# Two attention blocks on one core: another opening, zero matmuls, and the output projection from unit 40 at 2.5 matmuls a unit

## The chip, the cores and the metric

The kernel runs on one core of a Trainium2 chip. The time is that of one execution on the device, in microseconds; a kernel's time is the median of its runs. The profile is one further execution, taken by the hardware profiler. Its engines are TensorE (PE, with its weight loads PEld), VectorE (DVE), ScalarE (ACT), GpSimd (POOL) and SyncE (SP); SPq and POOLq are the queues in which SyncE and GpSimd issue DMAs.

## The reference

Two independent problems A and B of the same shape, with their own inputs, all bf16. For each, 16 batches of 144 query rows of width 448, 16 heads of width 256, and a cache of 512 keys and values per batch and head:

```python
q = (x @ wq).reshape(B, Sq, H, Dh).transpose(0, 2, 1, 3)      # x 16x144x448, wq 448x4096
scores = jnp.einsum("bhqd,bhkd->bhqk", q, k_cache) * (Dh ** -0.5)
p = softmax(scores, axis=-1)
o = jnp.einsum("bhqk,bhkd->bhqd", p, v_cache)
y = o.transpose(0, 2, 1, 3).reshape(B, Sq, H * Dh) @ wo       # wo 4096x448
out = concatenate([y_A, y_B], axis=-1)
```

## The kernel before

**Units.** A unit is one batch and one head of one problem; there are 2 x 16 x 16 = 512, in order of problem, batch and head. A unit goes through these steps, each named in the code by a letter pair and the unit's number:

- Q: eight matmuls of 128x144 make the unit's queries, transposed, in one PSUM bank (`t_q`); ScalarE or VectorE scales them into `qt_sb` (`t_evac_q`). Q of unit u stands `LQ` = 15 slots ahead of the unit.
- SA: two matmuls of 112x512 make the scores of the first 112 query rows, in one of two banks `sa_ps` (`t_sa`). VectorE takes the negated maximum (L436), ScalarE the exponential with its sum (L447), VectorE the reciprocal (L457), GpSimd multiplies (L465). Then TA: four transposes through TensorE into the same bank (`t_ta`), which VectorE copies to `pt_sb` (L488). SA stands `LS` = 5 slots ahead of its unit, TA 2.
- SB: the remaining 32 query rows of eight units are done together, in 16 small matmuls into the two banks `sb_ps` (`t_sb`), once in eight slots, 7 slots ahead. Their softmax runs for four units at a time; TB are their transposes.
- PV: eight matmuls of 128x144 of values and probabilities into one of two banks `ot_ps` (`t_pv`); ScalarE copies the result into a ring of four chunks of 128 output rows (`t_evac_ot`).
- OP: the output projection of a chunk of 128 rows is 32 matmuls of 128x448 into `op_ps` (`t_op_piece`). A chunk is complete when all 16 heads of its batches are; there are 18 chunks for each problem. ScalarE copies a finished chunk to `ost_sb` and GpSimd issues its store (`t_store`). The two last chunks run in `op_ps` and `qp_ps` together, and VectorE copies the second.

**Order.** A loop over slots i writes every engine's instructions in one fixed order; slot i holds PV of unit i and the earlier steps of later units. `_Sched.add` records each instruction with what it reads and writes, and puts in the semaphore waits. Within a slot TensorE has Q, SB (once in eight), SA, TA, TB (twice in eight), PV, OP.

**How OP is dealt out.** A finished chunk's 32 matmuls go into a queue with the slot from which they may run (two slots after the unit that completes it). Each slot adds `OP_RATE` to a credit (18 x 32 / 256 = 2.25), and matmuls are taken in pairs while a credit of one is left. While both queues are empty the credit is capped at four. After a chunk's last matmul no further one of that queue is taken until two slots later (`op_hold`).

**Loads.** All loads are issued by SyncE, in the order of a list sorted by due slot (`dma_plan`): x (transposed, for four batches), Wq in four groups of four heads, K for eight units (2 MB, transposed by the DMA, three buffers), V for four units (1 MB, three buffers), Wo in eight groups of four row blocks. A load that would overwrite a buffer waits on SyncE for the last reader, and everything behind it in the list waits too. Before, the list begins: x0, three groups of Wq, K0, the fourth Wq, V0, K1, V1, V2, K2, a Wo group, V3, two Wo groups, V4, K3, and Wo goes on until K5. V9, V10, K6, V11 follow. Wo of problem B is loaded as the last chunk of A releases each group.

The lines that deal out OP and cap the credit:

```python
            if i >= 0:
                credit += OP_RATE
            ...
            for bank in ("op", "qp"):
                while fifo[bank] and fifo[bank][0][2] <= i and credit >= 1 and (bank == "qp" or i >= op_hold):
                    r, cs = pop_items(bank, i, OPP)
                    credit -= len(cs)
            ...
            if not fifo["op"] and not fifo["qp"]:
                credit = min(credit, 2.0 * OPP)
```

Of the kernel before, what the change touches and what calls it, by code (L numbers as in the profile page):

```python
# [122 lines left out]
def bass_concat_heads__mha_block_cached__gqa_block_cached__near_ridge_kernel(  # L123
# [38 lines left out]
    LSB = 7  # L162
    NK, NV, NXG = 3, 3, 3
# [3 lines left out]
    KR = 4  # L167
# [8 lines left out]
    with contextlib.ExitStack() as es:  # L176
# [29 lines left out]
        sem_names = list(COMPUTE)  # L206
# [23 lines left out]
        def t_ident():  # L230
# [7 lines left out]
            S.add(POOL, e2, reads=[("ones", 0)], writes=[("ident", 0)], name="ident")  # L238

# [63 lines left out]

        def t_q(U):
# [4 lines left out]
            hg = h // 4  # L309

            def e(t):
                ins = None
                for kc in range(4):
                    for dc in range(2):
                        c0 = h * DH + dc * 128
                        ins = t.matmul(qp_ps[:, dc * SQ:(dc + 1) * SQ], lhsT=wq_sb[:, kc, c0:c0 + 128],  # L316
                                       rhs=xt_sb[:, xsl, kc, xo:xo + SQ], start=(kc == 0 and dc == 0),
                                       stop=(kc == 3), skip_group_check=True)
                return ins
            S.add(PE, e, reads=[(("wq", hg), pr), ("wqz", 0), (("xt", xsl), XG)], writes=[("qp", ("q", U))],  # L320
                  banks=["qp"], name="Q%d" % U)

        def t_evac_q(U):
            sl = U % NQT
            src = qp_ps[:, 0:2 * SQ].rearrange("p (c q) -> p c q", c=2)
            if (U - LQ) % 8 in (2, 4, 6, 7):
                def e(v):
                    return v.tensor_scalar(qt_sb[:, sl, :, :], src, 1.0 / 16.0, None, op0=ALU.mult)  # L328
                S.add(DVE, e, reads=[("qp", ("q", U))], writes=[(("qt", sl), U)], banks=["qp"], name="eq%d" % U)
            else:  # L330
                def e(a):
                    return a.activation(qt_sb[:, sl, :, :], src, AF.Copy, scale=1.0 / 16.0)  # L332
                S.add(ACT, e, reads=[("qp", ("q", U))], writes=[(("qt", sl), U)], banks=["qp"], name="eq%d" % U)
# [5 lines left out]
        def t_sb(SG):  # L339
            ksl = SG % NK  # L340

            def e(t):
                ins = None
                for dc in range(2):
                    for jj in range(8):
                        U = 8 * SG + jj
                        j = jj % 4
                        ins = t.matmul(sb_ps[jj // 4][32 * j:32 * j + 32, :].rearrange("q (k r) -> q k r", k=KR),  # L348
                                       lhsT=qt_sb[:, U % NQT, dc, QA:SQ],
                                       rhs=kt_of(U, dc), start=(dc == 0), stop=(dc == 1),  # L350
                                       tile_position=(0, 32 * j))
                return ins
            S.add(PE, e, reads=[(("qt", (8 * SG + jj) % NQT), 8 * SG + jj) for jj in range(8)] + [(("kt", ksl), SG)],
                  writes=[(("sbb", 0), ("s", 2 * SG)), (("sbb", 1), ("s", 2 * SG + 1))], banks=["sb0", "sb1"],
# [115 lines left out]
        def t_ta(U):  # L470
            psl = U % NPA
            bank = U % 2
# [10 lines left out]
        def t_evac_pta(U):  # L483
            sl = U % NPT
            bank = U % 2
# [87 lines left out]
        def t_store(r):  # L573
            pr, row0, m = chunk_rows(r)
            sl = r % NOST

            def e(q):
                return q.dma_start(of[row0:row0 + m, pr * D:(pr + 1) * D], ost_sb[0:m, sl, :]).then_inc(
                    sems["ost%d" % sl], 16)
            S.add(POOL, e, reads=[(("ost", sl), r)], dma_sem="ost%d" % sl, name="st%d" % r)  # L580
# [4 lines left out]
        t_ident()  # L585
        dma_plan = []
# [4 lines left out]
        s_min = -LQ - 24  # L591
        for XG in range(NXGT):
            pr, j = divmod(XG, Bn // XB)
            u_first = pr * NU + j * XB * H
            dl = u_first - LQ
# [6 lines left out]
        for pr in range(NP):  # L602
            for hg in range(HG):
                dl = pr * NU + 4 * hg - LQ
                lo = pr * NU - H + 4 * hg + 3 - LQ + 1 if pr > 0 else s_min
                plan(lo, dl, 10 ** 6, t_load_wq, pr, hg)
        for wg in range(NWG):
            plan(s_min, H - 4 + 2 * wg, 10 ** 6, t_load_wo, 0, wg)
        for SG in range(NSG):
            dl = 8 * SG - LSB  # L610
            lo = 8 * (SG - NK) + 7 - LS + 1 if SG >= NK else s_min
            plan(lo, dl, 12, t_load_k, SG)
        for G in range(NG):
            dl = 4 * G
# [5 lines left out]
        for dl, sq, lo, lead, fn, args in dma_plan:  # L620
            _prev = max(_prev, lo, dl - lead)
# [20 lines left out]
        OP_RATE = float(NCH * NWO) / NU  # L642
# [16 lines left out]
        while True:  # L659
# [3 lines left out]
            sgi, ph = divmod(i + LSB, 8)  # L663
            do_sb = ph == 0 and 0 <= sgi < NSG
            ga, gb = 2 * sgi, 2 * sgi + 1
            ok = 0 <= sgi < NSG
            if ok and ph == 1:
                t_exp_b(ga)
            if ok and ph == 3:
                t_exp_b(gb)  # L670
            if ok and ph == 2:
                t_recip_b(ga)
                t_norm_b(ga)
            if ok and ph == 4:
                t_recip_b(gb)
                t_norm_b(gb)
# [131 lines left out]
```

## Time and profile before

| | |
|---|---|
| median of 3 runs | 1211.84 us (1211.61 to 1212.8) |
| the profiled execution | 1210.82 us |
| its span, first to last instruction | 1209.1 us |
| TensorE busy | 1174.4 us, 97% |
| VectorE, ScalarE, GpSimd busy | 770.1, 753.7, 678.5 us |
| moved by DMA | 294.15 MB, mean 243 GB/s |
| first Q, first SB, first PV start | 10.33, 23.69, 37.88 us |
| SB of units 8, 16, 24, 32, 40, 48, 56 start | 39.11, 56.49, 73.76, 94.47, 112.87, 132.48, 148.94 us |
| last matmuls, last stores issued | 1201.99, 1203.09 us |

SB(n) is the one for units 8n to 8n+7; it stands in slot 8n - 7. How to read it: the page has busy times of engines and the costliest groups; a list of waits says who waited for whom and how long in total and at most; the timeline gives the start and duration of an instruction or of several alike. A matmul's duration holds its passage through the array, so consecutive groups overlap, and their spacing by start times is what they take. A DMA view gives the time from issue to landing; start of the issue plus that time is the landing.

### The profile page before, as it was taken

The page shows a single profiled execution, that of the slowest core. Times are in us where ns is not written, and L with a number is a line of the kernel's source. Part 1 is how long each engine was busy: PE and PEld are TensorE (multiplying, and loading weights), DVE is VectorE, ACT ScalarE, POOL GpSimd, SP SyncE. Part 2 cuts the span into 40 slices and gives each one's busy share as a digit, 9 for nine tenths or more (in the row PEclk, how much of TensorE's full clock was granted, in tenths as well). Part 3 has the DMA queues.
Part 4 walks back from the last instruction along what each step waited for, and adds up shares of the span by engine and source line. Part 5 has one row for each costly group of instructions (what it writes and reads, how often), then busy time and mean ns, then how long its engine had stood idle before and what let it go on. Part 6 is the DMA issues. An engine that isn't in the chain of part 4 may idle for free.

```text
span 1209.1 us, 33868 instructions
## 1 busy us (share of the span) xinstructions
PE 1174.4 (97%) x13952; PEld 894.2 (74%) x13952; DVE 770.1 (64%) x2179; ACT 753.7 (62%) x2213; POOL 678.5 (56%) x682
## 2 busy tenths in 40 slices
PE   4898999999999999999999999999999999999997
PEld 3676777777777777777777777777777777777765
DVE  1765666666666666666666666666666666666563
ACT  1665666666666666666666666666666666666553
POOL 0555565565555565565555655655655655665553
PEclk9999999999999999999999999999999999999999
DMA  9999999999999999999999999998999999999971
GB/s 249 281 285 289 245 252 225 245 251 247 246 235 237 231 259 226 246 246 232 290 283 282 284 272 265 228 258 225 245 244 236 224 249 244 242 240 234 232 178 47
DMA packets 627033, 294.15 MB, mean 243 GB/s; under 512 B 548416, under 2 KB 556608, under 8 KB 626880
## 3 DMA queue, kind: packets, MB, share of 16 engines
q1 hardware_dynamic: 625152, 287.85, 101.8%
q0 software_dynamic: 1728, 4.13, 1.1%
q8 instruction: 111, 1.82, 0.6%
q14 instruction: 42, 0.34, 0.1%
HBM read 148.90 MB, written 4.13 MB: 127 GB/s over the span
## 4 chain that ended last, share of the span: by engine, by line
PE 90%; DMA 5%; DVE 3%; SPq 1%; ACT 0%; issue 0%; POOL 0%; ACTq 0%
PE qp_ps L316 20%; PE ot_ps L511 19%; PE sa_ps L424 19%; PE op_ps L549 17%; PE sa_ps L478 8%; PE sb_ps L348 5%; DMA kt_sb<-in_A_k_cache_dram 3%; PE sb_ps L401 2%; DMA kt_sb<-in_B_k_cache_dram 2%; DVE stat L436 1%; DMA wq_sb<-in_A_wq_dram 0%; DVE pt_sb L488 0%; PE qp_ps L549 0%; DVE pt_sb L410 0%; DVE qt_sb L328 0%
## 5 line engine op out<-in xcount | busy, mean ns | idle before, releaser
L465 POOL TENSOR_TENSOR pa_sb<-pa_sb,stat 112x512 bf16<-112x512 bf16 x512 | 531.8, 1039 | 490.8 <-DVE stat L457 490.7
L447 ACT ACTIVATE pa_sb<-sa_ps,stat 112x512 bf16<-112x512 f32 x512 | 352.1, 688 | 408.0 <-DVE stat L436 407.0
L436 DVE TENSOR_REDUCE stat<-sa_ps 112x1 f32<-112x512 f32 x512 | 353.9, 691 | 324.6 <-PE sa_ps L424 321.1
L316 PE MATMUL qp_ps<-xt_sb,wq_sb 128*128 128x144 bf16 x4096 | 344.1, 228 | 16.1 <-DMA wq_sb<-in_A_wq_dram 10.3
L316 PEld LDWEIGHTS qp_ps<-xt_sb,wq_sb 128*128 128x128 bf16 x4096 | 290.5, 99 | 93.1 <-issue 11.1
L511 PE MATMUL ot_ps<-pt_sb,v_sb 128*128 128x144 bf16 x4096 | 340.4, 226 | 0.0
L424 PE MATMUL sa_ps<-kt_sb,qt_sb 128*112 128x512 bf16 x1024 | 310.9, 385 | 1.0 <-DVE pt_sb L488 0.8
L549 PE MATMUL op_ps<-wo_sb,ring 128*128 128x448 bf16 x1120 | 278.8, 352 | 0.0
L511 PEld LDWEIGHTS ot_ps<-pt_sb,v_sb 128*128 128x128 bf16 x4096 | 268.5, 97 | 0.4
L478 PEld LDWEIGHTS sa_ps<-ident,pa_sb 112*128 112x128 bf16 x2048 | 145.0, 97 | 111.3 <-ACT pa_sb L447 24.9
L526 ACT ACTIVATE ring<-ot_ps 128x288 bf16<-128x288 f32 (+8 forms) x512 | 190.3, 372 | 4.4 <-PE ot_ps L511 4.4
L488 DVE COPY pt_sb<-sa_ps 128x448 bf16<-128x448 bf16 x512 | 190.7, 372 | 2.4 <-PE sa_ps L478 2.4
L478 PE MATMUL sa_ps<-ident,pa_sb 112*128 112x112 bf16 x2048 | 185.4, 212 | 0.1
L328 DVE TENSOR_SCALAR qt_sb<-qp_ps 128x288 bf16<-128x288 f32 x256 | 117.0, 457 | 96.5 <-PE qp_ps L316 93.9
L389 POOL TENSOR_TENSOR pb_sb<-pb_sb,stat 128x512 bf16<-128x512 bf16 x128 | 132.8, 1037 | 27.1 <-DVE stat L381 27.1
L332 ACT ACTIVATE qt_sb<-qp_ps 128x288 bf16<-128x288 f32 x256 | 106.0, 414 | 35.0 <-PE qp_ps L316 32.5
L424 PEld LDWEIGHTS sa_ps<-kt_sb,qt_sb 128*112 128x112 bf16 x1024 | 97.0, 129 | 38.8 <-issue 26.7
L549 PEld LDWEIGHTS op_ps<-wo_sb,ring 128*128 128x128 bf16 x1120 | 95.1, 98 | 27.6 <-ACT ring L526 0.2
L447 ACT ACTIVATION_READ_ACCUMULATOR pa_sb<-sa_ps,stat 112x1 f32 x512 | 98.9, 193 | 0.0
L361 DVE TENSOR_REDUCE stat<-sb_ps 128x1 f32<-128x512 f32 x128 | 87.2, 681 | 3.7 <-PE sb_ps L348 3.7
L371 ACT ACTIVATE pb_sb<-sb_ps,stat 128x512 bf16<-128x512 f32 x128 | 88.5, 691 | 0.0
L457 DVE RECIPROCAL stat<-stat 112x1 f32<-112x1 f32 x512 | 78.4, 153 | 0.5 <-ACT pa_sb L447 0.5
(23 smaller groups left out, 366.1 us busy)
## 6 DMA issues: line engine op xcount, KB each, us to landing
v_sb<-in_A_v_cache_dram SPq DMA_DIRECT2D x64, 1024.0 KB, 6.1
v_sb<-in_B_v_cache_dram SPq DMA_DIRECT2D x64, 1024.0 KB, 6.0
out_dram<-ost_sb POOLq DMA_DIRECT2D x36, 112.0 KB, 5.1
wo_sb<-in_A_wo_dram SPq DMA_DIRECT2D x8, 448.0 KB, 6.3
wo_sb<-in_B_wo_dram SPq DMA_DIRECT2D x8, 448.0 KB, 6.2
wq_sb<-in_A_wq_dram SPq DMA_DIRECT2D x4, 768.0 KB, 6.7
wq_sb<-in_B_wq_dram SPq DMA_DIRECT2D x4, 768.0 KB, 7.6
wq_sb<-in_A_wq_dram SPq DMA_DIRECT2D x4, 128.0 KB, 6.9
```

What stands on the lines that cost most here:

```text
L316: ins = t.matmul(qp_ps[:, dc * SQ:(dc + 1) * SQ], lhsT=wq_sb[:, kc, c0:c0 + 128], rhs=xt_sb[:, xsl, kc, xo:xo + SQ], start=(kc == 0 and dc ...
L328: return v.tensor_scalar(qt_sb[:, sl, :, :], src, 1.0 / 16.0, None, op0=ALU.mult)
L389: return g.tensor_tensor(pb_sb[:, psl, :], pb_sb[:, psl, :], stat[:, RINVB + sl:RINVB + sl + 1].to_broadcast([128, SK]), op=ALU.mult)
L424: ins = t.matmul(sa_ps[bank][0:QA, :].rearrange("q (k r) -> q k r", k=KR), lhsT=qt_sb[:, U % NQT, dc, 0:QA], rhs=kt_of(U, dc), start=(dc = ...
L436: return v.tensor_reduce(stat[0:QA, NEG + sl:NEG + sl + 1], sa_ps[bank][0:QA, :], axis=AX.X, op=ALU.max, negate=True)
L447: return a.activation(pa_sb[0:QA, psl, :], sa_ps[bank][0:QA, :], AF.Exp, bias=stat[0:QA, NEG + sl:NEG + sl + 1], scale=1.0, accum_out=stat ...
L465: return g.tensor_tensor(pa_sb[0:QA, psl, :], pa_sb[0:QA, psl, :], stat[0:QA, RINV + sl:RINV + sl + 1].to_broadcast([QA, SK]), op=ALU.mult)
L478: ins = t.transpose(pta_ps[bank][:, c * 128:c * 128 + QA], src[:, c, :], ident[0:QA, 0:QA])
L488: return v.tensor_copy(pt_sb[:, sl, :, 0:QA], pta_ps[bank][:, 0:512].rearrange("p (c q) -> p c q", c=4)[:, :, 0:QA])
L511: ins = t.matmul(ot_ps[ob][:, dc * SQ:(dc + 1) * SQ], lhsT=v_sb[:, vsl, j, c * DH + dc * 128:c * DH + (dc + 1) * 128], rhs=pt_sb[:, sl, c, ...
L526: ins = a.activation(ring[:, 2 * h:2 * h + 2, c0:c0 + n1], src[:, :, 0:n1], AF.Copy)
L549: ins = t.matmul(acc[0:m, 0:D], lhsT=ring[:, c, col0:col0 + m], rhs=wo_sb[:, c, :], start=(c == first), stop=(c == last))
```

## The change

- The loads begin with x0, two groups of Wq, K0, the two other groups of Wq, V0, V1, V2, K1, K2. The first slot is now -9 instead of -39, and these loads carry due slots below -50, which puts them first.
- Q of the first 32 units no longer stands 15 slots ahead of its unit, but in slots of a table (`q_slot`): eight in slot -6, four in -3, four in -1, the others in 4 to 16. The first eight use four PSUM banks in turn (`qp_ps`, `op_ps` and the two `ot_ps`), the next 24 use `qp_ps` and `op_ps`. SB0, SB1 and SB2 move to slots -5, 4 and 10, SA of unit 8 to slot 4.
- Twelve zero matmuls of 128x512 stand before the first Q (W0) and 28 between the eighth Q and SB0 (W1). They read the identity and a part of `pt_sb` that VectorE clears, and write a bank that SB0 overwrites.
- Loads of problem A's Wo are due from slot 36 on, 1.7 slots apart, instead of from slot 12 on, 2 apart. In the list three groups stand between K5 and K6 (with V9 and V10), two more before V11, and three after V11.
- Chunks of problem A may run from unit 40 on; those of B as before. `OP_RATE` is 10/9 of what it was, 2.5.
- The two last stores are issued by SyncE, behind its last load, instead of GpSimd, with semaphores of their own, and SyncE waits for them at its end.

```diff
+    OP_FROM = (40, 0)
+    N_WARM = (12, 28)
...
+        def t_warm_zero():
+            def e(v):
+                return v.memset(pt_sb[:, 0, :, :], 0.0)
+            S.add(DVE, e, writes=[("warm", 0)], name="warmz")
...
+        def q_bank(U):
+            four = ((qp_ps, "qp", "qp"), (op_ps, "opp", "op"), (ot_ps[0], ("otp", 0), "ot0"),
+                    (ot_ps[1], ("otp", 1), "ot1"))
+            if U < 8:
+                return four[U % 4]
+            return four[U % 2] if U < 32 else four[0]
...
+        def t_warm(k):
+            def e(t):
+                ins = None
+                for _ in range(N_WARM[k]):
+                    ins = t.matmul(sb_ps[1][:, :], lhsT=ident[:, :], rhs=pt_sb[:, 0, :, 0:128], start=True, stop=True)
+                return ins
...
-            S.add(POOL, e, reads=[(("ost", sl), r)], dma_sem="ost%d" % sl, name="st%d" % r)
+            S.add(SP if r in tail_chunks else POOL, e, reads=[(("ost", sl), r)], dma_sem=sem, name="st%d" % r)
...
+        sb_slot = [8 * n - LSB for n in range(NSG)]
+        sb_slot[0:3] = [-LS, 4, 10]
+        sa_slot = [u - LS for u in range(NT)]
+        sa_slot[8] = 4
+        q_slot = [u - LQ for u in range(NT)]
+        q_slot[0:32] = [-6] * 8 + [-3] * 4 + [-1] * 4 + [4, 5, 5, 6, 7, 8, 9, 9] + \
+            [10, 11, 11, 12, 13, 14, 15, 16]
...
-        s_min = -LQ - 24
+        s_min = -LS - 4
...
-                dl = pr * NU + 4 * hg - LQ
+                dl = pr * NU + 4 * hg - LQ if pr > 0 else (-59, -58, -56, -55)[hg]
...
-            plan(s_min, H - 4 + 2 * wg, 10 ** 6, t_load_wo, 0, wg)
+            plan(s_min, OP_FROM[0] - 4 + 1.7 * wg, 10 ** 6, t_load_wo, 0, wg)
...
-            dl = 8 * SG - LSB
+            dl = 8 * SG - LSB if SG > 2 else (-57, -51, -50)[SG]
...
-            dl = 4 * G
+            dl = 4 * G if G > 2 else -54 + G
...
-        OP_RATE = float(NCH * NWO) / NU
+        OP_RATE = 10.0 / 9 * NCH * NWO / NU
...
+            if i == q_slot[0]:
+                t_warm(0)
+            for u in q_at.get(i, ()):
                 t_q(u)
                 t_evac_q(u)
+            if i == q_slot[0]:
+                t_warm(1)
...
-                            queue_chunk(r, i + OP_DELAY)
+                            queue_chunk(r, max(i + OP_DELAY, pr * NU + OP_FROM[pr]))
...
+                if eng_name == SP:
+                    for k in range(len(tail_chunks)):
+                        eng.wait_ge(sems["ostt%d" % k], 16)
```

## The prediction

> **What bounds the kernel now.** I read the page's shares first, then TensorE's waits and the DMA queue's own, then the timeline where TensorE is full and where it is not.
>
> ```profile
> PE 1174.4 (97%) x13952; PEld 894.2 (74%) x13952; DVE 770.1 (64%) x2179; ACT 753.7 (62%) x2213; POOL 678.5 (56%) x682
> DMA  9999999999999999999999999998999999999971
> ```
>
> TensorE and DMA both look full, so the waits must say which one ends last. TensorE's waits (total, times, longest):
>
> ```profile
> PE qp_ps L316 <- DMA wq_sb<-in_A_wq_dram: 10.3, 1, 10.3
> PE sb_ps L348 <- DMA kt_sb<-in_A_k_cache_dram: 6.1, 4, 1.9
> PE sb_ps L348 <- DMA kt_sb<-in_B_k_cache_dram: 2.9, 2, 2.2
> ```
>
> SyncE's queue, which issues every load:
>
> ```profile
> SPq L301 <- PE op_ps L549: 239.3, 58, 12.8
> ```
>
> After the start TensorE waits 9.0 us in all for K, in the opening (56 to 113 us) and at the change of problem, while the loads wait 239 us for TensorE to free V buffers. So the opening is bound by loads, the rest by TensorE's order. Three consecutive units there, by the start of PV:
>
> ```profile
> 158.74 0.66 PE L511 MATMUL ot_ps<-pt_sb,v_sb 128*128 128x144 bf16 x8
> 160.75 0.67 PE L511 MATMUL ot_ps<-pt_sb,v_sb 128*128 128x144 bf16 x8
> 162.76 0.67 PE L511 MATMUL ot_ps<-pt_sb,v_sb 128*128 128x144 bf16 x8
> ```
>
> 2.01 us a unit, with two out-projection matmuls. The chain of waits gives these a price, 4.16/22 = 0.189 us each:
>
> ```profile
> 1170.32 4.16 PE op_ps L549 x22
> ```
>
> So a unit without out-projection has 2.01 - 0.378 = 1.632 us of TensorE work. A stretch without any (1150 to 1168 us) shows what such a unit takes:
>
> ```profile
> 1160.50 0.64 PE L424 MATMUL sa_ps<-kt_sb,qt_sb 128*112 128x512 bf16 x2
> ...
> 1162.28 0.64 PE L424 MATMUL sa_ps<-kt_sb,qt_sb 128*112 128x512 bf16 x2
> ```
>
> ```profile
> 1161.18 0.69 DVE L436 TENSOR_REDUCE stat<-sa_ps 112x1 f32<-112x512 f32 x1 [0.33 <-PE sa_ps L424]
> 1161.85 0.38 DVE L488 COPY pt_sb<-sa_ps 128x448 bf16<-128x448 bf16 x1
> ```
>
> 1.78 us. SA feeds VectorE's maximum, the copy that frees the other score bank stands behind that maximum on VectorE, and the next SA waits for the copy: 0.64 + 0.61 + 0.07 + 0.38 and the hand-overs. This loop is a floor: an empty unit costs TensorE 1.78 - 1.632 = 0.148 us of idling, while a unit with out-projection covers it. The first empty unit after a full one takes 1.69, 0.055 over. Check: the sixteen units whose SB stand at 148.94 and 185.00 took 36.06 us with 32 out-projection matmuls and one run of six empty units; the same work at the dense rate (18.02 us per eight units with 18) is 35.28, and 0.055 + 5 x 0.148 = 0.80 makes up the rest.
>
> The end, by the lines of the epilogue:
>
> ```profile
> L176 SPq DRAIN  x1: 128/128/128, 1178.7 to 1178.7; - x1
> L176 POOLq DRAIN  x1: 3006/3006/3006, 1205.9 to 1205.9; - x1
> ```
>
> The last stores, issued by GpSimd at 1203.09, land at 1205.6; only then does GpSimd drain, and the drain ends the span.
>
> **The change, part by part.**
>
> *Opening: order of loads, banks, zero matmuls.* K0 stands ahead of the third Wq group instead of behind it: it landed at 7.34 + 16.2 = 23.6 and moves up by that group's 2.9 (landings 13.5 and 16.4), to 20.7. SB0 starts then, 3 us earlier. The third and fourth Wq then land at about 25 and 28 (the fourth came 4.4 behind K0, a group takes 2.9). Three V at 2.7 to 3.7 now stand before K1, which landed at 39.0 and moves to 43 to 46; K2 has the same loads ahead of it as before and stays near 56. Four banks remove the waits of Q for one bank (3.1 + 2.6 us). The zero matmuls (12 and 28, of 512 columns; SA's pair holds the array 0.43 us, so 0.215 each) take 2.6 and 6.0 us, twice that at the slow rate seen in the opening, where eight Q matmuls show 1.14 us and later 0.67. The first batch lies in the 10.3 us before Wq, the second before K0; slow, it holds SB0 to 31.5. The memset that they read is 288 words wide, an eighth of 2048 in the 1.76 us row: 0.25 us on an idle VectorE. I cost all this at nothing. What hides it is first the wait for K1, then a longer one at unit 40; without that cover it would be worth -3 to +8 us, as SB0 moves.
>
> *Wo from unit 36.* Eight Wo loads (1.15 us each between landings) leave the stretch before K5. K5 landed at 94.03 + 18.7 = 112.7 and moves to about 103.5.
>
> *Out-projection from unit 40.* Between SB1 and unit 40 every unit is now empty: 15.8 us per eight with SB (1.11) and two TB (0.45). From K1 at 44.5, six units and eight Q make 13.5 (SB2 58), seven units and eight Q 14.5 (72.5), then 88.3 and 104.1 (SB5), so TensorE comes to unit 40 at about 118. Chunk 0 sits in the queue from unit 15, so the cap on the credit no longer applies and the credit grows by 2.5 a unit to over 60: all 32 matmuls of chunk 0 stand at unit 40, and all 32 of chunk 1 at unit 42. Chunk 0 needs all eight Wo groups. SyncE issues three before K6, two after it, three after V11. Up to the last of them the set of loads is exactly the one that the kernel before had issued up to V11, which landed at 125.31 + 6.0 = 131.3, with the DMA engines never idle until then. The last Wo group therefore lands at 131.3 as well, and TensorE stands 6 to 7 us in the middle of chunk 0, with SB6 and all later units queued behind.
>
> Chunk 0 then ends near 132, and SB6 starts at 132.5, where it starts now (132.48). But by then the kernel before has done 58 out-projection matmuls, the changed one 32: 26 x 0.189 = 4.9 us of work is moved out of a stretch where TensorE had waited for loads anyway. By SB7 both have done 64: 8 x 1.632 + 1.11 + 0.45 + 32 x 0.189 + 0.85 for seven empty units = 21.5, so SB7 at 154.0 against 148.94. **+5.0 us.** Ends: -3.3 if loads run at the best rates of the rows (first rival); +9.1 if SyncE is held once on the way by a V buffer that isn't free (239.3 us in 58 waits, 4.1 each). I take the equal set of loads, since no such wait stands before 125 us now.
>
> *Rate 2.5 instead of 2.25.* A chunk is ready every sixteen units. Before: 10, 4, 2, 2, 2, 2, 2, 2, 2, 4 matmuls and six empty units; after: 12, 2, 2, 4, 2, 2, 2, 4, 2 and seven. Every eighth batch adds a ninth chunk, whose backlog fills some hundred units at 2.25 and about fifty at 2.5; then the empty runs return. Counted in the recorded orders, units 50 to 497 hold 31 first empty units in either kernel, and 42 later ones before, 110 after. 68 x 0.148 = **+10.1 us**. Ends: 68 x 0.055 = +3.7 by the first-unit row; 10.1 itself, which I take, because these stand second to seventh in their runs, as the units of the row do. Nothing offsets it: total out-projection work is equal.
>
> *Stores of the two tail chunks from SyncE.* GpSimd ends with its last multiplication near 1197 and drains before the stores land; SyncE waits for both, and its drain is 0.13 us. 3.0 - 0.13 = **-2.9 us**, if a store from SyncE lands 2.0 us after issue as GpSimd's does. Ends: 0, if SyncE's drain with stores behind it is as long as GpSimd's, and -3.4. The Trainium skill, "DMA: Bandwidth & Descriptors", section Specifications, gives a first byte after about 1 us for DMAs of GpSimd and 0.6 for SyncE's; by that the term would be -3.3 and the sum 11.8. No row here has a store from SyncE.
>
> **Sum.** 5.0 + 10.1 - 2.9 = +12.2 us. The profiled execution took 1210.82 (span 1209.1 and 1.7 around it), so 1223.0; the median of the runs is 1.0 above it, so **1224.0**.
>
> **The rivals.**
> - A: the opening isn't held by Wo. Rows for it: K took 7.2 us between landings at best, V 2.7; seven K, twelve V, eight Wo and Wq would be in by 111. Then K1 43.3, SB5 102.2, SB6 124.1, SB7 145.6: -3.3 in place of +5.0, total +3.9, 1215.7. Against it: in the same queue K took 8.5 to 9.9 whenever V and K alternated.
> - B, on the other side: loads, not TensorE's order, set the pace everywhere. DMA's row of nines speaks for it, SyncE's 239 us of waits against. Then where out-projection stands costs nothing, both positive terms go, and K2, with fewer changes between kinds of load, may come 1.4 early: -1.4 - 2.9 = -4.3, 1207.5. It decides once loads need more than 18.0 us per eight units; K to K with two V was 15.1 (landings 112.7 and 127.9).
> - C: the stall at unit 40 makes TensorE slow again. In the opening eight Q and SB0 (1.90 against 1.05) and one more Q lost 9 x 0.47 + 0.85 = 5.1 us so. Once more after the stall: 1229.1. Against it: SBs after waits of 1.5 to 1.9 us took 1.05. The Trainium skill, "TensorE: Matmul & The Clock Gate", section "HAM oscillation", says that idle gaps over about 3.4 us bring the slow clock back; by that, an estimate, 3.4 us at half rate, +1.7. The trace agrees that the opening is slow and later short waits are not.
>
> **How the numbers follow.** My forecast 0.79, A 0.08, B 0.06, C 0.07. A measurement of this kernel tells 0.2% (2.4 us) from no change. B is faster (0.05, and 0.01 so weak that it is same); 0.03 of A and of my forecast with the steady term at its low end fall within: faster 0.05, same 0.04, slower 0.91. Range 1215 to 1230: from A to C with the late Wo.
>
> **What would show it.** A wait of OP in unit 40 for Wo, ending near 131; SB6 near 132.5 and SB7 near 154; runs of seven empty units at 1.78; no POOL drain behind the stores. The forecast is wrong if Wo is in before unit 40, if empty units take 1.63, or if SB comes to wait for K throughout.

## The result, and the profile after

The changed kernel took 1233.87 us (median of six runs, 1229.02 to 1235.92), the kernel before, run beside it, 1212.43 (1211.61 to 1215.53): 1.017 times as long, 95% interval 1.0149 to 1.019. The profiled execution of the changed kernel took 1233.81 us, its span is 1232.1. Forecast were 1224.0 and a range up to 1230: the sign was right, the size was not.

The page of the changed kernel shows hardly more than before: TensorE full, DMA full. New is what the second line below shows, the granted TensorE clock in tenths: it falls below nine in the slice from 123 to 154 us, where the kernel before had nine throughout.

```profile
PE 1198.5 (97%) x13992; PEld 895.2 (73%) x13992; DVE 771.1 (63%) x2180; ACT 747.5 (61%) x2213; POOL 677.1 (55%) x680
PEclk9999899999999999999999999999999999999999
DMA  9999989999999999999999999999999989989971
```

TensorE's waits and the queue of SyncE (total, times, longest):

```profile
PE sb_ps L373 <- DMA kt_sb<-in_A_k_cache_dram: 7.0, 2, 4.4
PE op_ps L572 <- DMA wo_sb<-in_A_wo_dram: 4.8, 3, 3.0
PE sb_ps L373 <- DMA kt_sb<-in_B_k_cache_dram: 4.0, 2, 3.9
...
SPq L308 <- PE op_ps L572: 202.5, 47, 12.8
```

The wait for Wo is new and was forecast. The waits for K are 11.0 us instead of 9.0, fewer and longer. Where the time went is read from the start of PV of a unit in both traces. The stretches from one unit to another (us):

| stretch | before | after | difference | forecast |
|---|---|---|---|---|
| start to unit 44 | 140.5 | 149.6 | +9.1 | +5.0 |
| 44 to 236 | 433.8 | 437.9 | +4.1 | +4.3 |
| 236 to 272 (change of problem) | 84.3 | 93.1 | +8.8 | +0.5 |
| 272 to 490 | 497.0 | 501.4 | +4.4 | +5.1 |
| 490 to 511 | 44.8 | 44.8 | 0.0 | |
| last PV to the end | 8.74 | 5.15 | -3.6 | -2.9 |

The forecasts of the second to fourth row are the 10.1 us of the term for the rate, dealt out by where its empty units lie (what is missing to 10.1 is rounding and the units about 490). The differences add up to 22.8, the spans differ by 23.0 (the medians by 21.4). Two rows hold the miss.

The steady stretches look as the prediction read them: 2.01 us for a unit with out-projection, 1.78 for an empty one, in rows of seven. PV of two full units, and SA of two empty ones, in the timeline (start, duration):

```profile
170.28 0.67 PE L534 MATMUL ot_ps<-pt_sb,v_sb 128*128 128x144 bf16 x8
172.29 0.67 PE L534 MATMUL ot_ps<-pt_sb,v_sb 128*128 128x144 bf16 x8
...
188.64 0.64 PE L447 MATMUL sa_ps<-kt_sb,qt_sb 128*112 128x512 bf16 x2
190.42 0.64 PE L447 MATMUL sa_ps<-kt_sb,qt_sb 128*112 128x512 bf16 x2
```

Chunk 0 and chunk 1, on TensorE's timeline, with the idle time ahead of a group in brackets:

```profile
121.74 2.43 PE L572 MATMUL op_ps<-wo_sb,ring 128*128 128x448 bf16 x12
125.81 0.93 PE L572 MATMUL op_ps<-wo_sb,ring 128*128 128x448 bf16 x4 [1.64 <-DMA wo_sb<-in_A_wo_dram]
126.97 0.93 PE L572 MATMUL op_ps<-wo_sb,ring 128*128 128x448 bf16 x4 [0.23 <-DMA wo_sb<-in_A_wo_dram]
130.86 4.66 PE L572 MATMUL op_ps<-wo_sb,ring 128*128 128x448 bf16 x12 [2.96 <-DMA wo_sb<-in_A_wo_dram]
136.41 1.15 PE L373 MATMUL sb_ps<-kt_sb,qt_sb 128*32 128x512 bf16 x16
140.44 6.22 PE L572 MATMUL op_ps<-wo_sb,ring 128*128 128x448 bf16 x32
```

Twelve out-projection matmuls take 2.43 us in the first line and 4.66 in the fourth: behind the stall TensorE runs at half rate, for 6.8 us by the trace's clock record at 129.8. SB6 starts at 136.41; 132.5 was forecast.

At the change of problem the SBs of units 248, 256 and 264:

```profile
600.39 1.47 PE L373 MATMUL sb_ps<-kt_sb,qt_sb 128*32 128x512 bf16 x16 [4.41 <-DMA kt_sb<-in_A_k_cache_dram]
622.54 1.05 PE L373 MATMUL sb_ps<-kt_sb,qt_sb 128*32 128x512 bf16 x16 [0.18 <-DMA kt_sb<-in_B_k_cache_dram]
642.26 1.90 PE L373 MATMUL sb_ps<-kt_sb,qt_sb 128*32 128x512 bf16 x16 [3.85 <-DMA kt_sb<-in_B_k_cache_dram]
```

Before, TensorE waited there for the second and the third only, 2.91 us in all, and each SB took 1.05:

```profile
604.55 1.05 PE L348 MATMUL sb_ps<-kt_sb,qt_sb 128*32 128x512 bf16 x16 [2.19 <-DMA kt_sb<-in_B_k_cache_dram]
622.30 1.05 PE L348 MATMUL sb_ps<-kt_sb,qt_sb 128*32 128x512 bf16 x16 [0.72 <-DMA kt_sb<-in_B_k_cache_dram]
```

The windows of these 36 units, before and after, have the length, then the busy time of TensorE, its weight loads, VectorE, ScalarE and GpSimd, then the clock, the DMA share and GB/s:

```profile
574.26:658.53 84.27, 81.30 (x975) 62.50 (x973) 53.50 (x153) 52.40 (x151) 47.93 (x48) 1.00 1.14 284
587.57:680.71 93.14, 84.70 (x974) 63.28 (x972) 53.72 (x154) 51.61 (x150) 48.07 (x48) 0.96 1.09 262
```

So the 8.8 us have two parts. TensorE is idle for 8.4 us instead of 3.0, and it is busy for 3.4 us longer with the same work: behind the waits of 4.41 and 3.85 us the clock record shows half rate for 3.4 us each (from 600.9 and from 641.8), which costs 1.7 us each.

The end, by the lines of the epilogue:

```profile
L178 POOLq DRAIN  x1: 3752/3752/3752, 1221.7 to 1221.7; - x1
L178 SPq DRAIN  x1: 13/13/13, 1231.8 to 1231.8; - x1
```

GpSimd's drain is longer than before (3.75 us, it was 3.01), but ends 6.6 us ahead of the end.

### The profile page after: what moved, and what is told of

Read it like the earlier page. It is cut to its first block, busy times and chain, and to the rows that moved or that the text cites. A ratio compares the mean times of both kernels' runs of the same rounds, so it can differ in the third digit from the quotient of the medians.

```text
span 1232.1 us, 33950 instructions
## 1 busy us (share of the span) xinstructions
PE 1198.5 (97%) x13992; PEld 895.2 (73%) x13992; DVE 771.1 (63%) x2180; ACT 747.5 (61%) x2213; POOL 677.1 (55%) x680
## 3 DMA queue, kind: packets, MB, share of 16 engines
q8 instruction: 111, 1.82, 0.6%
## 4 chain that ended last, share of the span: by engine, by line
PE 88%; DMA 5%; DVE 3%; SPq 2%; issue 0%; ACT 0%; POOL 0%; DVEq 0%
PE sa_ps L447 19%; PE ot_ps L534 19%; PE qp_ps L331 18%; PE op_ps L572 17%; PE sa_ps L501 8%; PE sb_ps L373 5%; DMA kt_sb<-in_A_k_cache_dram 3%; PE sb_ps L424 2%; DVE stat L459 2%; DMA kt_sb<-in_B_k_cache_dram 2%; SPq L298 1%; DMA wo_sb<-in_A_wo_dram 1%; DVE pt_sb L511 1%; DVE pt_sb L433 1%; PE qp_ps L572 0%; SPq L288 0%
## 5 line engine op out<-in xcount | busy, mean ns | idle before, releaser
L331 PE MATMUL qp_ps<-xt_sb,wq_sb 128*128 128x144 bf16 x3952 | 328.8, 226 | 4.3 <-DMA wq_sb<-in_A_wq_dram 3.3
L331 PEld LDWEIGHTS qp_ps<-xt_sb,wq_sb 128*128 128x128 bf16 x3952 | 276.0, 98 | 62.3 <-DMA wq_sb<-in_A_wq_dram 4.3
L447 PE MATMUL sa_ps<-kt_sb,qt_sb 128*112 128x512 bf16 x1024 | 315.3, 390 | 1.9 <-DVE pt_sb L511 1.6
L572 PE MATMUL op_ps<-wo_sb,ring 128*128 128x448 bf16 x1120 | 267.6, 355 | 4.8 <-DMA wo_sb<-in_A_wo_dram 4.8
L501 PEld LDWEIGHTS sa_ps<-ident,pa_sb 112*128 112x128 bf16 x2048 | 139.9, 97 | 122.2 <-ACT pa_sb L470 49.8
L344 DVE TENSOR_SCALAR qt_sb<-qp_ps 128x288 bf16<-128x288 f32 x243 | 110.9, 456 | 85.6 <-PE qp_ps L331 84.6
L572 PEld LDWEIGHTS op_ps<-wo_sb,ring 128*128 128x128 bf16 x1120 | 98.5, 98 | 50.3 <-DMA wo_sb<-in_A_wo_dram 6.7
L412 POOL TENSOR_TENSOR pb_sb<-pb_sb,stat 128x512 bf16<-128x512 bf16 x128 | 133.2, 1041 | 0.0
L394 ACT ACTIVATE pb_sb<-sb_ps,stat 128x512 bf16<-128x512 f32 x128 | 88.7, 693 | 0.1
L373 PE MATMUL sb_ps<-kt_sb,qt_sb 128*32 128x512 bf16 x1024 | 69.2, 391 | 12.8 <-DMA kt_sb<-in_A_k_cache_dram 7.0
```

The lines of the kernel that those rows point to most:

```text
L331: ins = t.matmul(acc[:, dc * SQ:(dc + 1) * SQ], lhsT=wq_sb[:, kc, c0:c0 + 128], rhs=xt_sb[:, xsl, kc, xo:xo + SQ], start=(kc == 0 and dc = ...
L373: ins = t.matmul(dst.rearrange("q (k r) -> q k r", k=KR), lhsT=qt_sb[:, U % NQT, dc, QA:SQ], rhs=kt_of(U, dc), start=(dc == 0), stop=(dc = ...
L412: return g.tensor_tensor(pb_sb[:, psl, :], pb_sb[:, psl, :], stat[:, RINVB + sl:RINVB + sl + 1].to_broadcast([128, SK]), op=ALU.mult)
L447: ins = t.matmul(sa_ps[bank][0:QA, :].rearrange("q (k r) -> q k r", k=KR), lhsT=qt_sb[:, U % NQT, dc, 0:QA], rhs=kt_of(U, dc), start=(dc = ...
L501: ins = t.transpose(pta_ps[bank][:, c * 128:c * 128 + QA], src[:, c, :], ident[0:QA, 0:QA])
L572: ins = t.matmul(acc[0:m, 0:D], lhsT=ring[:, c, col0:col0 + m], rhs=wo_sb[:, c, :], start=(c == first), stop=(c == last))
```

## The experiments

The stretches of each kernel's own profile, and its runs. The last column is the ratio to the kernel before, run beside it (its medians were 1213.4 to 1214.6 for the experiments, 1212.43 for the changed kernel), where there were enough runs for an interval.

| kernel | to unit 44 | 44 to 236 | 236 to 272 | 272 to 490 | last PV to end | median us | ratio |
|---|---|---|---|---|---|---|---|
| before | 140.5 | 433.8 | 84.3 | 497.0 | 8.74 | 1212.43 | |
| after | 149.6 | 437.9 | 93.1 | 501.4 | 5.15 | 1233.87 | 1.0149 to 1.019 |
| e1, after at rate 2.25 | 149.8 | 433.8 | 88.4 | 497.0 | 5.15 | 1221.88 | 1.0047 to 1.008 |
| e2, before at rate 2.5 | 142.4 | 438.0 | 88.2 | 501.4 | 8.75 | 1225.86 | 1.0085 to 1.0113 |
| e3, only the new opening and tail | 139.3 | 433.7 | 91.5 | 498.5 | 5.15 | 1212.64 | 0.9977 to 1.0001 |
| e4, only the tail | 144.2 | 433.7 | 85.6 | 497.0 | 5.16 | 1210.85 | 0.996 to 0.9987 |
| e5, after, no credit until unit 40 | 133.8 | 452.1 | 93.0 | 501.5 | 5.14 | 1228.3 | 1.0097 to 1.0144 |
| e6, after without zero matmuls | 154.8 | 438.2 | 88.2 | 501.5 | 5.16 | 1230.56 | 1.0118 to 1.0163 |
| e7, after, stall filled | 147.0 | 438.0 | 86.1 | 501.5 | 5.15 | 1227.21 | 1.0084 to 1.0136 |
| e8, after, less of B's Wq | 149.8 | 438.0 | 82.8 | 501.5 | 5.17 | 1225.21 | 1.0082 to 1.0117 |
| e9, tail, fewer empty units | 139.8 | 429.5 | 84.8 | 496.2 | 5.16 | 1204.99 | 0.9913 to 0.9943 |
| e10, before again | 140.5 | 433.8 | 85.0 | 497.0 | 8.74 | 1211.49 | |
| e11, before again | 141.4 | 433.7 | 85.4 | 497.0 | 8.75 | 1212.88 | |
| e12, after again | 148.4 | 438.0 | 88.7 | 501.5 | 5.15 | 1228.27 | |
| e13, before with 40 matmuls in front | 138.1 | 433.7 | 89.8 | 497.0 | 8.74 | 1214.27 | 0.9992 to 1.0014 |
| e14, after with 88 more in W0 | 155.2 | 437.9 | 87.7 | 501.4 | 5.15 | 1231.18 | 1.012 to 1.016 |
| e15, before with 128 in front | 141.8 | 433.7 | 84.3 | 497.0 | 8.75 | 1212.1 | |
| e16, before with 64 in front | 139.9 | 433.7 | 91.6 | 498.3 | 8.75 | 1218.78 | |

A stretch in this table is that of one execution. The two steady stretches repeat within 0.3 us in kernels with the same work there (in e3 and e16 the second is 1.3 to 1.5 us longer, a further wait for K of 1.44 and 1.25 us), but the opening scatters: it took 140.5, 140.5 and 141.4 us in three profiles of the kernel before and 144.2 in e4, whose opening is the same. A difference of less than some 4 us in the first column therefore shows nothing by itself.

**e1 and e2: the rate undone, and the rate alone.**

```diff
-        OP_RATE = 10.0 / 9 * NCH * NWO / NU     # e1, in the changed kernel
+        OP_RATE = float(NCH * NWO) / NU
```

> The changed kernel with the credit rate of before, 2.25 matmuls a unit; all else as changed. Theory: the rate alone makes both the empty units (8.5 us from unit 44 to 490) and the waits for K around the change of problem (8.9 against 0.5 worked out, so 8.4 more). Then units 44 to 236 take 433.8 us as before, 236 to 272 84 to 85, and the time falls by about 17 to 1217. Rival: the waits around the change of problem come from the changed list of loads or from the whole run standing later, not from the rate; then units 236 to 272 stay near 92 and the time is about 1225.

> The kernel before with the credit rate 2.5 and nothing else. Theory: units 44 to 236 take 437.9 us, 272 to 490 501.4, and K is waited for around unit 240 and 256, so +17 us, 1229.5. Rival (rate makes empty units only): +8.5, 1221. If empty units cost nothing: 1212.4.

Both steady stretches go with the rate alone, whatever else the kernel has: 433.8 and 497.0 us at 2.25, 437.9 to 438.0 and 501.4 to 501.5 at 2.5. That is +8.5 us for empty units, where the prediction had put 9.4 of its 10.1. The theory put all that the change of problem lost on the rate, the rival nothing of it. Both medians lie between the two: with either half of the change the stretch from unit 236 to 272 takes some 4 us more than in the kernel before.

**e3: the opening's loads, banks and zero matmuls without the late Wo.** The changed kernel with rate 2.25, `OP_FROM = (0, 0)` and the plan for Wo of before.

> The changed kernel with the output projection and the Wo loads of before (rate 2.25, chunks from two slots after their last unit, Wo due from slot 12), so that the new opening and the new last stores are left. Theory: the opening is bound by the same set of loads, so it gains 0 to 2 us at unit 44; with 3.6 us at the end 1207 to 1209. Rival: the early units that the new opening saves (2.3 us at unit 0, and no slow clock) are kept to the end: 1205 or less. Rival on the other side: Q in the opening banks or the wait for K1 costs time once Wo loads stand there again: 1212 or more.

The opening is 1.2 us shorter (within its scatter) and the tail 3.6, as expected, and yet the median is only 0.9 below before, where 1207 to 1209 was expected: its profile loses 7.2 us from unit 236 to 272. TensorE has in this kernel from unit 44 on the same instructions in the same order as in the one before, so neither the rate nor the order of its work there can be the cause.

**e4: the tail alone.**

```diff
-            S.add(POOL, e, reads=[(("ost", sl), r)], dma_sem="ost%d" % sl, name="st%d" % r)
+            S.add(SP if r in tail_chunks else POOL, e, reads=[(("ost", sl), r)], dma_sem=sem, name="st%d" % r)
```

> The kernel before with the two last stores issued by SyncE and nothing else. Theory: the stretch from the last PV to the end falls from 8.75 us to 5.2, so 1212.4 - 3.6 = 1208.8. Rival: the 3 us of draining on GpSimd are waited for by something else at the end, 1212.4.

-3.6 us at the end by the trace, -2.7 by the medians. The opening of this profile is 3.7 us longer than before without any change there.

**e5: the stall at unit 40 without the burst.** The credit stays capped at four until unit 40, so that out-projection comes two to four matmuls a unit from there.

```diff
-            if not fifo["op"] and not fifo["qp"]:
+            if (not fifo["op"] and not fifo["qp"]) or i < OP_FROM[0]:
                 credit = min(credit, 2.0 * OPP)
```

> The changed kernel, but the credit stays capped at four until unit 40, so that the two chunks held back run off at 2.5 matmuls a unit and chunk 0 meets its Wo groups as they land, instead of 32 matmuls in unit 40 and 32 in unit 42. Theory (the burst is what waits for Wo and cools TensorE): no wait for Wo above 1 us, no half-rate record between 125 and 140; SB7 then waits for K7 (landed 148.3) instead; units 45 to 236 have 25 empty units instead of 64, worth 5.9 us. Some 36 matmuls (7 us) move from before unit 49 to after it. Sum -10 + 7 - 6 = -9, about 1225. Rival (the loss in the opening is moved work alone, not the stall): the time stays within 3 us of 1234.

The wait for Wo is gone and unit 44 starts at 133.8. But the next load is late instead, K7, which lands behind all the Wo groups; SB7 on the timeline:

```profile
151.23 1.90 PE L373 MATMUL sb_ps<-kt_sb,qt_sb 128*32 128x512 bf16 x16 [7.23 <-DMA kt_sb<-in_A_k_cache_dram]
```

Unit 236 starts at 585.9, against 587.6 in the changed kernel: of 15.8 us gained at unit 44 1.7 are left, since the work that had been done under one stall now stands behind the other. The medians differ by 5.6, with wide runs in both: 1228.3 lies between the two expectations, nearer the first. The opening is bound by its loads, and by how much out-projection is done while TensorE waits for them.

**e6: no zero matmuls.** W0, W1 and the memset are left out.

> The changed kernel without the 40 zero matmuls and the memset that they read. Theory: Q and SB0 run at half rate again, but TensorE waits for K1 until 44.5 and for Wo until 133 in any case, so the time is the changed kernel's, 1234 within 2 us, with unit 0 up to 4 us later and unit 33 at the same time. Rival (the zero matmuls are a gain that the rest of the change hides): 1238 or more.

Nothing is lost: 1230.56, 3.3 below the changed kernel where 1234 within 2 was expected. The opening is 5.2 us longer in the profile, the change of problem 4.9 shorter (the changed kernel, profiled once more, came to 88.7 there itself, e12). What zero matmuls in the first 22 us have to do with that stretch is what e13 to e16 tell.

**e7: the stall kept busy.** Matmuls of 128 columns on constants (28 and 48) stand where chunk 0 waits for Wo, so that the wait is the same but TensorE isn't idle.

```diff
+                    if r == 0 and cs[-1] in (11, 19):
+                        t_fill(100 + cs[-1], {11: 28, 19: 48}[cs[-1]])
```

> The changed kernel with 28 and 48 more matmuls of identity and ones, 128 columns each, in the two places of chunk 0 where TensorE waits for Wo (1.64 and 2.96 us); their result is overwritten by SB6. Theory: the half-rate record of 6.8 us at 130 goes, the last twelve matmuls of chunk 0 take 2.3 us instead of 4.5 and Q and SB6 0.6 less, so SB6 starts 2.5 to 3.4 us earlier than 136.4 and the time falls by 3, to 1231. Rival (the half rate is not caused by the idling there): the record stays and nothing is gained, or the time grows by what the matmuls take beyond the wait.

The clock record at 130 is gone, and the groups behind the wait take 0.93 us for four, as at full rate, paced by the loads:

```profile
126.99 2.84 PE L368 MATMUL sb_ps<-ones,ident 128*128 128x128 bf16 x48
130.11 0.93 PE L581 MATMUL op_ps<-wo_sb,ring 128*128 128x448 bf16 x4 [0.28 <-DMA wo_sb<-in_A_wo_dram]
...
133.87 1.05 PE L382 MATMUL sb_ps<-kt_sb,qt_sb 128*32 128x512 bf16 x16
```

SB6 starts at 133.87 instead of 136.41, unit 44 at 147.0 instead of 149.6. Of these 2.5 us, 0.75 are an earlier landing of the last Wo group (132.46, not 133.21); SB6 starts 1.4 us behind that landing instead of 3.2, so the half rate costs 1.8 us. That is a third of the prediction's rival C (5.1). It is close to the 1.7 that the prediction estimated from the Trainium skill, "TensorE: Matmul & The Clock Gate", section "HAM oscillation". The median is 6.7 lower, of which the opening explains a third or so; the change of problem (86.1) is shorter again.

**e8: the change of problem with less to load.** Of each group of B's Wq the large part loads 64 of its 1024 columns; B's queries are then made from what stands in the buffer.

```diff
+                few = slice(hg * 4 * DH, hg * 4 * DH + 64) if pr else cols
-                q.dma_start(wq_sb[:, 0:3, cols], ...
+                q.dma_start(wq_sb[:, 0:3, few], ...
```

> The changed kernel with most of problem B's Wq not loaded (64 of 1024 columns of each group's large part; 2.9 of 3.7 MB left out, so problem B's output is not the reference's). It measures what the loads of the change of problem cost. Theory: units 236 to 272 are bound by loads there; without them they take 81.7 to 84 us instead of 93.1, K is not waited for, no half-rate record at 600 to 656, and the time falls by 9 to 11, to 1224. Rival (K waits because the V buffers of the empty run are freed late, whatever is loaded besides): the wait at unit 240, ahead of which only one of the four Wq groups stands, remains at about 4 us and the time falls by less than 5.

10.3 us are gone from the 93.1 of the changed kernel (82.8; 5.9 against e12's 88.7), and with them all waits for K but one of 1.14. So this stretch is bound by loads: the extra time there comes from loads that land later, not from the order of TensorE's work.

**e9: fewer empty units.** The kernel before with the tail of e4, rate 2.15 and no credit kept over empty queues.

```diff
-        OP_RATE = float(NCH * NWO) / NU
+        OP_RATE = 2.15
...
-                credit = min(credit, 2.0 * OPP)
+                credit = min(credit, 0.0)
```

> The kernel before with its two last stores on SyncE, OP_RATE 2.15 instead of 2.25 and no credit kept while both queues are empty. Played through by the loop that deals out the work, units without out-projection between 44 and 490 fall from 29 first and 39 later ones to 31 first and 22 later ones less 4, so the loss by 0.055 and 0.148 us falls by some 5 us if the counts are priced as in the prediction (from about 9.4 to 4.2 us). Theory (an empty unit idles TensorE wherever loads do not decide): 1213.4 - 3.3 (stores, mean of the -2.7 and -3.6 measured) - 5.1 = 1205, with the trace's stretch from unit 44 to 236 shorter by about 2 us and that from 272 to 490 by about 2. Rival (the gain is given back where loads decide, at the change of problem): 1210.

1204.99 us, 0.9928 times before (0.9913 to 0.9943): faster than both kernels, and the expected total. The parts are not as expected, so that the total came out right by luck in part: -4.3 and -0.8 in the two steady stretches, -3.6 in the tail, and +3.1 between units 490 and 511, where what the lower rate left over is done. In the profiles the lower rate thus gains 2.0 us, not 5.1, and the spans differ by 5.7, while the medians differ by 9.6 (before, run beside it, had 1214.61, and its profile is of an execution of 1210.82). The other 4 us were not traced.

**e10, e11, e12: both kernels once more**, unchanged.

> The kernel before, unchanged, profiled once more. Theory (the stretch from unit 236 to 272 is paced by loads that do not take the same time in each execution): 36 units there in 84 to 91 us, other than the 84.3 of the first profile by 2 us or more in at least one of two such profiles. Rival (the stretch is as fixed as the others, and the longer ones of the experiments come from their edits): 84.3 within 1.

> As for the other copy of the kernel before: 84 to 91 us from unit 236 to 272 by the theory, 84.3 within 1 by the rival.

> The changed kernel, unchanged, profiled once more. Theory: the opening to unit 44 within 2 us of 149.6 and the two steady stretches within 0.5 us of 437.9 and 501.4, while the stretch from unit 236 to 272 may be anywhere in 86 to 93 us. Rival (the faster rate alone sets it): 93.1 within 1.

The kernel before repeats itself: 84.3, 85.0 and 85.4 us from unit 236 to 272. My theory, that the loads there vary by chance, fell for it. The changed kernel took 93.1 and 88.7, so it isn't fixed, but was more in both profiles. Something in the program decides, and e1, e3, e6 and e7 say that it is neither the rate alone nor the work there.

**e13 to e16: instruction fetches.** The DMA view counts 111 packets of 16 KB in the queue for instructions, 1.82 MB, and 112 in the kernels with 64 or more matmuls more (e7, e14, e15, e16). TensorE has 13952 matmuls and as many weight loads, so by division, if this queue serves TensorE alone, a fetch holds some 250 instructions, 126 matmuls; that 64 to 128 more matmuls add one packet agrees. In the trace most come every 10 to 12 us. Where a fetch falls among the loads depends on how many instructions TensorE has had, and the change puts forty matmuls (W0 and W1) in front. e13, e15 and e16 add nothing else to the kernel before; e14 is the changed kernel with W0 made of 100 zero matmuls of 64 columns instead of twelve of 512, so that it has 128 more than e6.

```diff
+                    ins = t.matmul(sb_ps[0][:, 0:32], lhsT=ident[:, :], rhs=ones[:, 0:32], start=True, stop=True)
...
+        t_fill(40)      # e13; 64 in e16, 128 in e15
         i = s_min
```

> The kernel before with 40 matmuls of 32 columns put in front of the first Q, where TensorE waits for Wq; nothing else. Theory (TensorE's instructions are fetched in pieces of 16 KB, one for each 128 matmuls, some 12 us apart; forty matmuls more shift every later fetch to another place among the loads, and one that falls into the transposed load of K31 delays it): from the issue of the V load ahead of problem B's x to the landing of K31 21.2 us or more instead of 20.2 to 20.5, and units 236 to 272 take 87 to 91 us instead of 84.3 to 85.4; the median 2 to 5 us above before. Rival (the fetches do not matter; the new opening's order of loads does): 20.2 to 20.5, 84.3 to 85.5, median within 1.

> The changed kernel with W0 made of 100 zero matmuls of 64 columns instead of twelve of 512, so that it has 128 matmuls more than without zero matmuls: just one fetch of 16 KB. Theory: the fetches stand again as in the kernel without zero matmuls, from the V load to K31's landing 20.3 to 20.9 us instead of 23.4, units 236 to 272 take 86 to 88.5 instead of 88.7 to 93.1, the median 2 to 5 us below the changed kernel's 1233.9. Rival: 23.4, and 88.7 or more.

> The kernel before with 128 matmuls of 32 columns in front of the first Q, one whole fetch. Theory: as the kernel before, 20.2 to 20.6 us to K31's landing and 84.3 to 85.6 for units 236 to 272. Rival (more matmuls at the start cost there by themselves): as with forty, or more.

> The kernel before with 64 matmuls of 32 columns in front of the first Q, half a fetch. Theory: the fetches lie half a period, some 6 us, off those of the kernel before, so that one falls into the middle of K31's load: 21 us or more to its landing, 86 or more for units 236 to 272. Rival: 20.2 to 20.5 and 84.3 to 85.5.

In the old kernel the stretch goes with the place of the fetches: 84.3 to 85.4 us with none or 128 matmuls more, 89.8 with 40, 91.6 with 64, in one profile each but for none. In the new one the sign is the same, but the gap is small beside the scatter: 86.1 to 88.2 (e6, e7, e14) against 88.7 and 93.1. In the windows of the trace the stretch has the same instructions. The kernel before with 128 matmuls more:

```profile
575.50:659.90 84.40, 81.36 (x977) 62.57 (x975) 53.53 (x153) 52.33 (x151) 47.93 (x48) 1.00 1.14 284
```

With 40 and with 64 (one line of each kernel's windows):

```profile
571.90:661.70 89.80, 82.64 (x976) 62.91 (x974) 53.47 (x153) 52.35 (x151) 47.98 (x48) 0.98 1.11 267
```

```profile
573.60:665.20 91.60, 84.16 (x976) 63.77 (x974) 53.47 (x153) 52.33 (x151) 47.93 (x48) 0.96 1.09 265
```

TensorE is idle for 3.0, 7.2 and 7.4 us in these three windows; the rest of the difference is the clock (1.00, 0.98, 0.96). In every run listed the stretch is 80 to 82 us, plus the waits for K, plus 1.7 us for each 3.4 us at half rate. With 40 more, TensorE waits 1.22 us for K31, 3.02 for K32 and 2.92 for K33.

The DMA view of 20 us in slices of half a microsecond, from 6 us after the issue of B's first x, shows what a fetch does to K31, whose transposed load moves 290 GB/s. With 128 more, the fetch falls on the end of K31, at 17.8 us after x:

```profile
GB/s 219 8 9 105 319 393 381 389 325 219 265 290 288 291 289 291 290 290 291 288 291 289 291 261 86 332 369 377 201 315 401 389 385 389 385 381 340 254 332 393
```

With 40 more it falls at 15.1, while K31 runs:

```profile
GB/s 5 20 288 285 347 336 356 352 371 250 108 275 289 287 186 285 289 291 308 42 4 10 252 290 290 290 291 300 74 123 356 401 439 371 403 406 406 410 426 348
```

"42 4 10 252" in place of four times 290 is 1.5 us in which hardly anything moves. K31 lands 21.6 us after the issue of the V load ahead of x, with 128 more 20.2. In the other kernels, by the place of the fetch 14 to 20 us after x, the second one behind it (in e16 the first, the one ahead lies 0.4 us before x), and K31's landing counted so (e8 loads less here and is left out):

| second fetch at | kernels | K31 lands after |
|---|---|---|
| 17.8 to 18.1 | before, e10, e11, e15, e4, e2, e6, e7 | 20.2 to 20.6 |
| 18.0 | e14 | 21.3 |
| 15.1 to 16.0 | e1, e3, e13 | 21.3 to 21.6 |
| 15.1 to 16.0 | after, e12, e5, e16 | 23.0 to 23.5 |
| 19.3, the first at 7.6 | e9 | 21.8 |

Why the same place costs 1.2 us in some kernels and 3 in others isn't settled. The fetch ahead of it lies 5.0 to 5.1 us after x in the third row and at 4.7 or earlier in the fourth; no run varied that alone.

e14 brings the changed kernel to 87.7 us in that stretch, within what was expected, and its opening is slower (155.2), so its median moved only by 2.7. Two expectations missed. K31 in e14 lands 0.4 later than the band given. And e13's median is 0.6 above before, not 2 to 5: its stretch is 5.5 longer, but its opening 2.4 shorter, because from unit 0 to 33 it takes 72.4 us instead of 76.6 (76.3 to 78.1 in e10, e11 and e4; 128 matmuls more leave 76.5). It may be that the fetches fall elsewhere among the opening's loads too, there to its advantage; that isn't shown. So what fetches cost at the change of problem stands in the profiles, and e13's runs show no loss in total.

## Why the prediction was wrong

- **"+5.0 us" for the opening was mis-sized: it is +9.1** (4.2 to 9.3 over all profiles of the two openings). The mechanism was the one forecast: the last Wo group holds chunk 0 in unit 40, with SB6 behind it. The equal set of loads put that group at 131.3; it landed at 133.2 (+1.9). And chunk 0 did not run on at full rate behind it: its last 12 matmuls took 4.66 us instead of 2.4, and the Q behind them 1.17, so that SB6 started 1.8 us later than at full rate (e7). Rival C was kept apart with a chance of 0.07 because waits of 1.5 to 1.9 us had left the clock alone; the stall forecast was 6 to 7 us, in which I should have taken the half rate as the likelier case. TensorE came to unit 40 at 121, not 118, as it had waited 2.6 us for K1 and run at half rate behind that too; this only shortened the stall, to 4.8 us in three waits.
- **The change of problem was no term of the sum at all: it is +8.8 in the profile** (+4.4 in the second). The prediction read that TensorE waits for K there, and then costed only empty units in it. By the windows it is 5.5 us more waiting for K and 3.4 us lost to the half rate behind those waits. Where loads decide, everything that shifts them counts. What shifted them is in part the forty zero matmuls: they move TensorE's instruction fetches into the transposed K loads (e13 to e16, e6). "I cost all this at nothing" holds for the opening, within its scatter, and fails 570 us later. Another part, some 2.5 us, goes with the rate: at 2.5 and with the fetches in the old place (e2, e6, e7, e14) the stretch takes 86.1 to 88.2, at 2.25 (before, e10, e11, e15, e4) 84.3 to 85.6. Most of that is waiting for K again: 4.3 to 4.9 us at 2.5, 2.0 to 3.0 at 2.25. 0.5 of it was worked out for empty units. Why K comes late for the faster rate wasn't settled.
- **"+10.1 us" for the rate: right, a tenth too large.** +8.5 in the two steady stretches against 9.4 worked out for them; e1 and e2 show that the rate alone makes it.
- **"-2.9 us" for the stores: right in its mechanism, -3.6 by the trace.** From the issue of the last stores to the end it takes 2.7 us (1229.38 to 1232.1) instead of 6.0, and the issue stands 0.3 nearer to the last PV. The two stores land 1.7 us after their issue, GpSimd's took 1.9 and 2.0. The Trainium skill, "DMA: Bandwidth & Descriptors", section Specifications, by which the term came out at -3.3, is nearer than the -2.9 taken.
- **Rival A** (not held by Wo) and **rival B** (loads set the pace everywhere) fell: the wait for Wo stands in the trace, and the steady stretches follow the rate. But B was right for a place, the 36 units at the change of problem.
- Summed by the trace, the change loses 9.1 by its late output projection, 8.5 by empty units, 8.8 at the change of problem, and wins 3.6 at the end. The forecast's three terms were each of the right sign; what carried the time out of its range is the half rate and the change of problem.

## What to carry to other kernels

Where two engines both look full, divide the span into stretches by their last wait and price a change in each; a stretch that waits for loads is moved by anything that touches the DMA engines, and a stall of several microseconds is to be priced with the slow clock behind it. A kernel whose instruction stream is fetched while it runs has the place of its fetches among the loads set by the count of instructions ahead, so 6 to 9% of a load-bound stretch (5 to 7 of 84 us in the profiles here) can come or go with 40 to 64 matmuls hundreds of microseconds earlier: compare against a copy padded to a whole fetch before a cause is named. Work that fills an engine's idle floor (two matmuls in each slot) is worth spreading thin, not fast: of the rates 2.15, 2.25 and 2.5 the lowest, in e9, took least time in the steady stretches, and gave 3.1 of its 5.1 us back at the end by the profiles. e9 changed the credit kept over empty queues too, and the two weren't parted.

## What the runs showed of the hardware that was not expected

- A fetch of 16 KB of instructions during a transposed K load can stop nearly all DMA traffic for some 1.5 us (290 to 4 GB/s in half-microsecond slices of e13), while its packet takes about 1 us on one of 16 engines. It doesn't always: in the profile before, 61 fetches begin while transposed loads move, and 37 of them are followed within 3 us by a microsecond below 50 GB/s; away from fetches that is so after 4 of 185 moments, taken 1 us apart, of such loads.
- Half rate came after shorter waits than the prediction's rows had shown: SB took 1.80 us behind a wait of 1.95 in e10, and 1.90 behind 2.12 in e9, but 1.05 behind 2.19 in the profile before. The Trainium skill, "TensorE: Matmul & The Clock Gate", section "HAM oscillation", gives idle gaps over about 3.4 us as the limit. Here 2 us were enough in some executions and not in others.
- At the end GpSimd's drain took 3.01 us where it had issued the last stores and 3.75 to 3.76 where SyncE had, in every profile; SyncE's took 0.13 and 0.01.
